# Chunked attention and gated feed-forward on one core: three tiles moved to transposing transfers, one load moved to another queue, a new order of loads, and eight equal blocks

## The chip, the core and the metric

The kernel runs on one core of one Trainium2 chip. The metric is the device time of one launch in microseconds (us). Each time is that of a whole execution; the profile shows one of them instruction by instruction.

## The reference

Two computations follow each other. The first is attention in chunks of 32 positions, for 4 batches, 8 heads, 768 positions and a head size of 64. A chunk sees 16 positions to its left, its own 32, 8 to its right, and 8 memory rows:

```python
for c in range(nc):
    l_start = max(0, c_start - left_ctx)          # 16
    r_end = min(S, c_end + right_ctx)             # 8
    k_full = np.concatenate([mem_k, k[:, :, l_start:r_end]], axis=2)
    v_full = np.concatenate([mem_v, v[:, :, l_start:r_end]], axis=2)
    scores = scale * np.matmul(q_c, k_full.transpose(0, 1, 3, 2))
    a = softmax(scores)
    out[:, :, c_start:c_end] = np.matmul(a, v_full)
```

The second takes the 3072 positions with their 512 features as `x` and gives the result:

```python
gate = np.maximum(x @ w_gate, 0.0)     # 512 -> 1536
val = x @ w_val
return (gate * val @ w_out).astype(np.float32)
```

## The kernel before

The 3072 positions are 24 tiles of 128 (`NT`), six to a batch (`TPB`). A tile goes through attention in these steps, whose names are the keys of the plan: `t` transposes q or k (TensorE, or a transposing transfer on SyncE's queue), `tc` or `kc` copies the result into place, `s` are the scores, `max`, `sub`, `exp`, `sum`, `rec`, `nrm` the softmax on VectorE and ScalarE, `p` transposes the probabilities, `pc` copies them out of PSUM, `v` multiplies with the values, and `x` copies the transposed attention result into `xT`, the input of the feed-forward part.

Tiles 0 to 5 load their q and k as three pairs (`load_pair`, names Q0 to K2); later tiles load them one by one (`load_qk`, names q6 to k23). `BY_DMA = (14, 15)` says from which tile on q and k are transposed by a transfer (`qk_dma`, L275) and no more by TensorE (`qk_t`, L266); `BY_DMA_P = 14` says it for p (`p_dma` L352, `p_t` L348). With a transfer, q lands in place, while k lands in a buffer `k_t` and is still copied by ScalarE. `scores` is L300, `values` L365.

The feed-forward part works on blocks of tiles: `BLOCKS` gives their sizes, seven blocks of three or four tiles. Within a block, `first` (L411) makes for each of twelve column groups `m` four products for the gate and four for the value; `relu` (ScalarE, L417) and `gate` (VectorE, L423) follow; then `second` (L432) makes twelve products for each tile, and the result is copied and stored. Blocks 0 and 1 are interleaved group by group while the weights still come.

Loads from memory that change the type go through GpSimd's queue in the order of the string `LOADS`: K and Q pairs, q and k, `v` with two digits (half of the chunks, head pair) for the values of batch 0, `b` with two digits (batch, head pair) for those of later batches, `w` for five groups of both weights, `o` for the output weights, `m` the memory values, `z` memsets of the second value buffer, `i` the identity matrix. The values lie in `v_bd`, of which there are two (`NSET`), used by batches in turn: batch 2 waits for the last values of batch 0, batch 3 for those of batch 1 (tile 11). The first half of batch 0's values comes by `v_parts` (L194), where the first chunk, which has no left context, is a load of its own.

The order of instructions on every engine is written by `schedule` (L704): a list plan with a duration for each step, priorities, and landing times for transfers. It only fixes orders; on the chip each instruction waits for what it needs. On one engine the instructions run in that order, so one that waits holds up those behind it. `LEAD` holds numbers that shape the priorities: entries 2 to 7 say how many column groups ahead of a block its attention may start (`pace`), the others order the copies of the memory pattern and the first tiles.

Of the kernel before, what the change touches and what calls it, by code (L numbers as in the profile page):

```python
# [16 lines left out]
ACT = mybir.ActivationFunctionType  # L17
# [4 lines left out]
def kernel(  # L22
# [12 lines left out]
    nc = tc.nc  # L35

    B, H, S, D = q.shape
    NMEM = mem_k.shape[2]
# [11 lines left out]
    KW = CH + NMEM  # L50
    CTX = 16 + CH + 8
    NSET = 2
    BLOCKS = [3, 3, 3, 4, 3, 4, 4]
    LEAD = [22, -5, 16, 12, 4, 3, 14, 23, 5, -6, 7, 17, 24, 4, 24, 12, 12, 0, 3, -6, -3]
    LAST = ((0, 384), (384, 512))
    BY_DMA = (14, 15)
    BY_DMA_P = 14
    LANDING = 3.0
    PAIRS = 3
    SPLIT = 1  # L60
# [2 lines left out]
    MEM_LEAD = (0,0,4,4)  # L63
    BY_DMA_X = 24
    BESIDE = 10.0
    LOADS = """K0 Q0 K1 i v01 Q1 Q2 K2 v00 v02 v03 w0 v12 w1 z1 v13 v11 w2 v10 w3
               m z3 w4 q7 q6 q8 z0 k8 k6 q9 k7 o1 k23 k9 o0 k13 z2 b13 b12 q13
               q21 k16 q12 b11 b10 k10 q17 k20 k11 q10 k18 q16 b21 q11 k15 q18 q14 k12 k14 b23
               b22 k21 k22 q15 b20 b30 q19 q20 q23 q22 b32 k17 b33 b31 k19"""

    KEY_RUNS = ((CH, KW, 0), (0, CH, NMEM), (KW, 64, KW))
    assert sum(BLOCKS) == NT and NMEM == 8 and D == 64 and H == 8
# [19 lines left out]
    def copy(eng, o, i):  # L92
        if eng is nc.scalar:
            nc.scalar.copy(o, i)  # L94
        else:
            eng.tensor_copy(o, i)
# [91 lines left out]
    def load_v_rows(b, par, hp, s0, s1, c0, c1):  # L188
# [2 lines left out]
            bass.AP(tensor=v.tensor, offset=v[b, 2 * hp + par, 0, 0].offset + (CH * c0 + s0 - 16) * D,  # L191
                    ap=[[D, s1 - s0], [CH * D, c1 - c0], [1, D]]))

    def v_parts(b, par, hp, c0, c1):  # L194
        parts = []
        if (b, par, hp, c0) == (0, 0, 0, 0):
            parts.append((b, par, hp, 16, CTX, 0, 1))
            c0 = 1
        if (b, par, hp, c1) == (B - 1, 1, HP - 1, NCH):
            c1 -= 1  # L200
            parts.append((b, par, hp, 0, 48, c1, c1 + 1))
        return parts + [(b, par, hp, 0, CTX, c0, c1)]
# [251 lines left out]
    def op(key, eng, fn, deps=(), prio=(0,), take=(), give=(), after=()):  # L454
        ops[key] = dict(eng=eng, fn=fn, deps=list(deps), prio=prio, take=list(take), give=list(give),
                        after=list(after))
# [4 lines left out]
    def psum(n):  # L461
# [3 lines left out]
    MARGIN = 1.2  # L465


    op("warm", {"DVE": 0.15}, lambda e: nc.vector.memset(warm, 0.0), prio=(-9,))
    op("warm2", {"ACT": 1.5}, lambda e: nc.scalar.activation(warm, warm, ACT.Exp), ["warm"], prio=(-9,), after=["vml"])  # L469
    op("vm00", {"DVE": 0.3}, lambda e: nc.vector.memset(vmem_0.rearrange("p h d -> p (h d)").bitcast(F32), 0.0),  # L470
       prio=(-8,), after=["im"])
    op("vml", {"ACT": 0.7}, lambda e: pattern_load(), prio=(-10,))
    op("kml", {"SP": 1.3}, lambda e: mem_load(), prio=(-8,))
    op("im", {"DVE": 0.12}, lambda e: nc.vector.memset(ident_h.bitcast(F32), 0.0), prio=(-8.5,), after=["warm"])
    op("ib", {"DVE": 0.25}, lambda e: nc.vector.tensor_copy(ident_b, ident_h), ["ident"], prio=(-7,))
# [45 lines left out]
    for a in range(NT):  # L521
# [52 lines left out]
        blk = block_of[a]  # L574
        j = a - starts[blk]
        ready = [("vl", b, 0 if b else t // 3, n) for n in range(2 * HP)]
        ready += [("mr", b, par, hp) for par in range(2) for hp in range(HP)] if b else []
        if a < BY_DMA_X:
            op(("v", a), {"PE": 0.41}, lambda e, a=a: values(a), [("pc", a)] + ready, (1, a, 10),
# [54 lines left out]
    def load_v_op(b, half, par, hp, c0, c1, deps, after):  # L634
        n = 2 * hp + par
        for i, part in enumerate(reversed(v_parts(b, par, hp, c0, c1))):
            rows = part[4] - part[3]
            load(("vl", b, half, n) if i == 0 else ("vx", b, n), rows * (part[6] - part[5]),
                 rows * (part[6] - part[5]) * 0.95e-3, lambda part=part: load_v_rows(*part), deps, (), after)

    def load_v_half(half, hp):
        c = NCH // 2
# [50 lines left out]
    def timed(d):  # L693
        return isinstance(d, tuple) and len(d) == 2 and isinstance(d[1], float)

    MOVE = {"t": 1.3, "p": 1.3, "x": 1.3, "mr": 0.7}

    LAG = 0.15

# [4 lines left out]
    def schedule():  # L704
# [30 lines left out]
        while len(started) < len(ops) + len(loads):  # L735
# [8 lines left out]
            while moved:  # L744
                moved = False
                for e in ("POOL", "PE", "ACT", "DVE", "SP"):
                    if free[e] > t + 1e-9:
                        continue
                    if e == "POOL":
                        if n_load == len(loads):  # L750
                            continue
                        o = loads[n_load]
                        if len(flying) >= 8 or not ready(o, t):
                            continue
                        n_load += 1
                        key = o["key"]
                        if o["n"]:
                            end = t + 0.62 + 0.27e-3 * o["n"]
                            queue_end = max(queue_end, end + 0.8) + o["work"]
                            load_end = queue_end + 1.0  # L760
                            flying.append(load_end)
                            done[key] = queue_end + (1.5 if n_load < 8 else 2.4 if n_load < 35 else 4.0)
                        else:
                            end = done[key] = t + o["work"]
                        if locked > t:
                            end += 0.25
                        fn = o["fn"]
                    else:
                        o = None
                        for _, key in todo[e]:  # L770
                            late_pe = e == "PE" and t > 36.0 and ops[key]["prio"][0] == 1
                            if ready(ops[key], t, MARGIN if late_pe else 0.0):
                                o = ops[key]
                                break
                        if o is None and e == "PE" and "ident" in done and 6.0 < t and ("f", 0, 0, 0) not in started:
                            order.append((t, idle_product))
                            free[e] = t + 0.1
                            heapq.heappush(times, free[e])
                            continue
                        if o is None:  # L780
                            continue
                        for x in o["eng"]:
                            todo[x].remove((o["prio"], key))
                        d = o["eng"][e] * (1.8 if e == "PE" and (t < 10.0 and key[0] == "t" or t < 24.0 and key[0] == "p") else 1.0)
                        if e == "DVE" and holds_port(key):
                            end = max(t + d, free["POOL"] + d - 0.1 if free["POOL"] > t else 0.0)
                            locked = end
                        else:
                            end = t + d
                        done[key] = end + (0.25 if e == "PE" else LAG)  # L790
                        if e == "SP" and key[0] in "tpx":
                            done[key] = end + (BESIDE if n_load < len(loads) or t < load_end else LANDING)
                        if e == "SP" and key[0] in MOVE:
                            queue_end = max(queue_end, t) + MOVE[key[0]]
                        fn = lambda o=o, e=e: o["fn"](e)
                        for g in o["give"]:
                            g, lag = g if isinstance(g, tuple) else (g, 0.0)
                            gives.append((done[key] + lag, g))
                            heapq.heappush(times, done[key] + lag)
# [47 lines left out]
```

## Time and profile before

| What | Value |
|---|---|
| Three runs | 239.75, 239.22, 237.85 us; median 239.22 |
| The profiled execution | 238.81 us, of which the span of the program is 237.0 |
| Granted TensorE clock | 1.00 |
| TensorE busy | 225.5 us, 2432 matmuls |
| VectorE busy | 150.9 us |
| ScalarE busy | 117.8 us |
| GpSimd busy | 91.5 us (issuing loads and setting memory) |
| Data moved by transfers | 27.17 MB |

The page of the profile gives the busy time of each engine, then the span in 40 slices with a digit for the busy tenths of each, then the queues, the chain of work that ended last, and groups of instructions by line, with the number of them, busy time, mean length, and the idle time of the engine before them with what ended it. A view by stage (windows) gives busy times between two moments. A view in order of time gives start and length of instructions; for matmuls the recorded length is more than the distance to the next, because they overlap.

### The profile page before, as it was taken

The page shows a single profiled execution, that of the slowest core. Times are in us where ns is not written, and L with a number is a line of the kernel's source. Part 1 is how long each engine was busy: PE and PEld are TensorE (multiplying, and loading weights), DVE is VectorE, ACT ScalarE, POOL GpSimd, SP SyncE. Part 2 cuts the span into 40 slices and gives each one's busy share as a digit, 9 for nine tenths or more (in the row PEclk, how much of TensorE's full clock was granted, in tenths as well). Part 3 has the DMA queues.
Part 4 walks back from the last instruction along what each step waited for, and adds up shares of the span by engine and source line. Part 5 has one row for each costly group of instructions (what it writes and reads, how often), then busy time and mean ns, then how long its engine had stood idle before and what let it go on. Part 6 is the DMA issues. An engine that isn't in the chain of part 4 may idle for free.

```text
span 237.0 us, 5892 instructions
## 1 busy us (share of the span) xinstructions
PE 225.5 (95%) x2432; PEld 125.6 (53%) x2432; DVE 150.9 (64%) x267; ACT 117.8 (50%) x251; POOL 91.5 (39%) x107
## 2 busy tenths in 40 slices
PE   0988989999999999999999999999999999999994
PEld 0777655665544666655444545664454444444442
DVE  5789953468999789954999146797775520234300
ACT  7988735444442786653643356655553331333212
POOL 6989998884875787059430000000000000000000
PEclk9999999999999999999999999999999999999999
DMA  7999999999999999979999344545420002200022
GB/s 75 163 160 179 161 180 179 165 192 172 151 174 211 199 179 133 118 127 149 141 150 117 75 149 111 69 46 121 127 48 0 0 4 88 88 0 0 3 88 89
DMA packets 121147, 27.17 MB, mean 115 GB/s; under 512 B 111264, under 2 KB 118176, under 8 KB 121120
## 3 DMA queue, kind: packets, MB, share of 16 engines
q0 software_dynamic: 101376, 16.61, 94.7%
q1 hardware_dynamic: 19664, 10.16, 18.5%
q8 instruction: 19, 0.31, 0.6%
q14 instruction: 8, 0.07, 0.1%
q10 hardware_dynamic: 80, 0.02, 0.0%
HBM read 33.24 MB, written 6.29 MB: 167 GB/s over the span
## 4 chain that ended last, share of the span: by engine, by line
PE 84%; POOL 8%; DMA 3%; ACT 2%; issue 1%; ACTq 0%; POOLq 0%
PE out_ps L432 26%; PE v_ps L411 25%; PE g_ps L411 25%; POOL v_bd L189 5%; PE xT_ps L365 4%; DMA v_bd<-in_v_dram 3%; PE s_ps L300 2%; PE qk_ps L266 2%; POOL w_gate_sb L121 1%; POOL w_val_sb L121 1%; POOL qk_p L220 1%; PE pT_ps L348 1%; ACT v_bd L94 1%; POOL v_bd L135 1%; ACT L469 1%
## 5 line engine op out<-in xcount | busy, mean ns | idle before, releaser
L423 DVE TENSOR_TENSOR gvT<-v_ps,g_relu 128x384 f16<-128x384 f32 (+1 forms) x84 | 51.2, 610 | 42.4 <-PE v_ps L411 42.0
L411 PE MATMUL v_ps<-xT,w_val_sb 128*128 128x384 f16 (+1 forms) x336 | 75.9, 349 | 0.3 <-DMA w_val_sb<-in_moe_w_val_dram 0.3
L411 PE MATMUL g_ps<-xT,w_gate_sb 128*128 128x384 f16 (+1 forms) x336 | 75.9, 349 | 0.0
L417 ACT ACTIVATE g_relu<-g_ps 128x384 f16<-128x384 f32 (+1 forms) x84 | 44.8, 534 | 57.9 <-PE g_ps L411 47.4
L432 PE MATMUL out_ps<-w_out_sb,gvT 128*128 128x512 f16 (+2 forms) x300 | 65.5, 370 | 0.0
L411 PEld LDWEIGHTS <-w_gate_sb 128*128 128x128 f16 x336 | 32.1, 98 | 28.1 <-DMA w_gate_sb<-in_moe_w_gate_dram 0.4
L411 PEld LDWEIGHTS <-w_val_sb 128*128 128x128 f16 x336 | 31.3, 98 | 26.8 <-DMA w_val_sb<-in_moe_w_val_dram 0.5
L189 POOL DMA_DIRECT2D v_bd<-in_v_dram x42 | 37.7, 910 | 16.6 <-PE xT_ps L365 9.3
L432 PEld LDWEIGHTS <-gvT 128*128 128x128 f16 x300 | 28.0, 98 | 30.0
L94 ACT COPY o_sb<-out_ps 128x512 f32<-128x512 f32 (+2 forms) x25 | 14.2, 569 | 32.8 <-PE out_ps L432 32.4
L164 DVE TENSOR_TENSOR v_bd<-vmem 8x768 int32<-8x768 int32 (+1 forms) x29 | 26.6, 944 | 1.1 <-ACT vmem L94 0.9
L327 ACT ACTIVATE p_exp<-dif 128x64 f16<-128x64 f32 (+2 forms) x72 | 19.6, 336 | 8.9 <-DVE dif L320 8.7
L313 DVE TENSOR_REDUCE mx<-s_ps 128x8 f32<-128x512 f32 x24 | 16.3, 677 | 5.5 <-PE s_ps L300 5.2
L331 DVE TENSOR_REDUCE sm<-p_exp 128x8 f32<-128x512 f16 x24 | 16.3, 678 | 5.2 <-ACT p_exp L327 5.1
L211 POOL DMA_DIRECT2D qk_b<-in_k_dram x18 | 16.0, 891 | 5.5 <-DMA w_out_sb<-in_moe_w_out_dram 2.8
L211 POOL DMA_DIRECT2D qk_b<-in_q_dram x18 | 16.0, 902 | 5.0 <-DMA v_bd<-in_v_dram 1.6
L342 DVE TENSOR_TENSOR p_n<-p_exp,rinv 128x512 f16<-128x512 f16 x24 | 16.4, 684 | 0.3
L320 DVE TENSOR_TENSOR dif<-s_ps,mx 128x512 f32<-128x512 f32 x24 | 16.4, 682 | 0.1
L365 PEld LDWEIGHTS <-v_bd 128*128 128x128 f16 x384 | 12.7, 96 | 5.2 <-issue 1.3
L365 PE MATMUL xT_ps<-pT,v_bd 128*128 128x32 f16 x384 | 13.0, 176 | 0.9 <-DMA v_bd<-in_v_dram 0.7
L94 ACT CAST xT<-xT_ps 128x512 f16<-128x512 f32 x17 | 9.9, 587 | 7.3 <-PE xT_ps L365 7.0
L403 PE MATMUL idle_ps<-ident_h 128*128 128x128 f16 x87 | 8.4, 238 | 4.8 <-POOL ident_h masks.py:199 4.8
(46 smaller groups left out, 125.5 us busy)
## 6 DMA issues: line engine op xcount, KB each, us to landing
out_dram<-o_sb SPq DMA_DIRECT2D x23, 256.0 KB, 2.1
v_bd<-in_v_dram POOLq DMA_DIRECT2D x23, 168.0 KB, 9.6
qk_b<-in_q_dram POOLq DMA_DIRECT2D x18, 128.0 KB, 9.3
qk_b<-in_k_dram POOLq DMA_DIRECT2D x18, 128.0 KB, 9.2
w_out_sb<-in_moe_w_out_dram POOLq DMA_DIRECT2D x2, 768.0 KB, 10.8
v_bd<-in_v_dram POOLq DMA_DIRECT2D x15, 84.0 KB, 4.9
qk_p<-in_k_dram POOLq DMA_DIRECT2D x3, 256.0 KB, 5.9
qk_p<-in_q_dram POOLq DMA_DIRECT2D x3, 256.0 KB, 5.3
```

The lines of the kernel that those rows point to most:

```text
L94: nc.scalar.copy(o, i)
L164: nc.vector.tensor_tensor(out=o, in0=i, in1=i, op=ALU.bitwise_or)
L189: nc.gpsimd.dma_start(v_bd[b % NSET][64 * par + NMEM + s0:64 * par + NMEM + s1, hp, c0:c1, D * par:D * par + D], bass.AP(tensor=v.tensor, ...
L211: nc.gpsimd.dma_start(qk_b[a, i], bass.AP(tensor=x.tensor, offset=x[b, 0, 128 * t, 0].offset, ap=[[D, 128], [S * D, H], [1, D]]))
L320: nc.vector.tensor_tensor(out=SM[a, "dif"].rearrange("p h r s -> p r h s"), in0=S_ps.pop(a), in1=mx_b, op=ALU.subtract)
L327: nc.scalar.activation(p[:, :, :, s0:s0 + k1 - k0], dif[:, :, :, k0:k1], ACT.Exp, scale=SCALE)
L342: nc.vector.tensor_tensor(out=P_n[a], in0=SM.pop((a, "p")), in1=rinv_b, op=ALU.mult)
L365: nc.tensor.matmul(ps[:, hp, r], lhsT=v_bd[b % NSET][:, hp, 4 * t + g, :], rhs=x[:, hp, r], start=True, stop=True)
L411: nc.tensor.matmul(ps, lhsT=w[:, f, 128 * m:128 * m + 128], rhs=xTs[blk][:, f, :], start=(f == 0), stop=(f == NFC - 1))
L417: nc.scalar.activation(st["r", m], st.pop((0, m)), ACT.Relu)
L423: nc.vector.tensor_tensor(out=st["gv"][:, m, :], in0=st.pop((1, m)), in1=st.pop(("r", m)), op=ALU.mult)
L432: nc.tensor.matmul(st["o", t, cols], lhsT=st["gv"][:, m, 128 * t:128 * t + 128], rhs=w_out_sb[:, m, slice(*cols)], start=(m == 0), stop=(m ...
```

## The change

- `BLOCKS` becomes eight blocks of three tiles.
- `BY_DMA` becomes (13, 13) and `BY_DMA_P` 12: q of tile 13, k of tiles 13 and 14, and p of tiles 12 and 13 are transposed by transfers on SyncE's queue.
- The first chunk's 40 rows of v for head 0 come as float32 by SyncE's queue (`load_first`) into rows 24 to 63 of `vmem_f`, the buffer that already takes the memory rows; a memset clears rows 0 to 31 before (`vf0`), and a copy on ScalarE or VectorE (`vfc`) writes rows 0 to 63 into the first chunk of `v_bd`. GpSimd's load of these rows is gone. The load of the memory rows and the memset `warm` now come after `vf0`; the values of tile 0 wait for `vfc`.
- The plan assumes later landing: 2.7 us in place of 2.4 after a load's turn in the queue (for loads 8 to 34), transposing transfers that take 1.45 in place of 1.3 of queue time, rows of v 1.0 in place of 0.95 ns per row, and a load that counts as in flight until 0.2 us after its assumed landing.
- `LOADS` and `LEAD` hold other orders and numbers.

```diff
-    BLOCKS = [3, 3, 3, 4, 3, 4, 4]
-    LEAD = [22, -5, 16, 12, 4, 3, 14, 23, 5, -6, 7, 17, 24, 4, 24, 12, 12, 0, 3, -6, -3]
+    BLOCKS = [3, 3, 3, 3, 3, 3, 3, 3]
+    LEAD = [24, 8, 20, 20, 11, 11, 4, 7, 10, 5, 4, 24, 17, 0, 24, 3, 22, 1, -6, -6, 7]
...
-    BY_DMA = (14, 15)
-    BY_DMA_P = 14
+    BY_DMA = (13, 13)
+    BY_DMA_P = 12
...
-    LOADS = """K0 Q0 K1 i v01 Q1 Q2 K2 v00 v02 v03 w0 v12 w1 z1 v13 v11 w2 v10 w3
-               m z3 w4 q7 q6 q8 z0 k8 k6 q9 k7 o1 k23 k9 o0 k13 z2 b13 b12 q13
-               q21 k16 q12 b11 b10 k10 q17 k20 k11 q10 k18 q16 b21 q11 k15 q18 q14 k12 k14 b23
-               b22 k21 k22 q15 b20 b30 q19 q20 q23 q22 b32 k17 b33 b31 k19"""
+    LOADS = """K0 Q0 i K1 K2 Q1 v01 v00 Q2 v11 v03 v02 w0 v13 v12 w1 v10 w2 q6 k7
+               w3 z2 z3 z1 q7 k6 b12 m k8 q9 w4 k16 o0 q8 k9 o1 b11 z0 q10 q17
+               k23 k15 k10 b10 b13 k19 k14 k11 q11 k13 k18 q15 q14 k12 q13 k17 q20 q12 b21 b22
+               q21 k22 k21 k20 q19 b33 b20 b23 q16 b32 q18 b31 q23 b30 q22"""
...
+    def load_first():
+        nc.sync.dma_start(
+            vmem_f[NMEM + 16:64, 0, 0:D],
+            bass.AP(tensor=v.tensor, offset=v[0, 0, 0, 0].offset, ap=[[D, 64 - NMEM - 16], [1, D]]))
...
         if (b, par, hp, c0) == (0, 0, 0, 0):
-            parts.append((b, par, hp, 16, CTX, 0, 1))
             c0 = 1
...
-    op("warm", {"DVE": 0.15}, lambda e: nc.vector.memset(warm, 0.0), prio=(-9,))
+    op("vf0", {"DVE": 0.1}, lambda e: nc.vector.memset(vmem_f[0:32, 0, 0:D], 0.0), prio=(-10,))
+    op("warm", {"DVE": 0.15}, lambda e: nc.vector.memset(warm, 0.0), prio=(-9,), after=["vf0"])
...
+    op("vfl", {"SP": 0.4}, lambda e: load_first(), ["vf0"], prio=(-7.5,), after=["kml"])
+    op("vfc", {"ACT": 0.15, "DVE": 0.15}, lambda e: copy(engine[e], v_bd[0][0:64, 0, 0, 0:D], vmem_f[0:64, 0, 0:D]),
+       [("vfl", 3.2), ("vml", 1.2), ("spread", 0, 0)], prio=(1, 0, 9))
...
-    op("vml", {"ACT": 0.7}, lambda e: pattern_load(), prio=(-10,))
+    op("vml", {"ACT": 0.7}, lambda e: pattern_load(), ["vf0"], prio=(-10,))
...
+        ready += ["vfc"] if a == 0 else []
...
-                 rows * (part[6] - part[5]) * 0.95e-3, lambda part=part: load_v_rows(*part), deps, (), after)
+                 rows * (part[6] - part[5]) * 1.0e-3, lambda part=part: load_v_rows(*part), deps, (), after)
...
-    MOVE = {"t": 1.3, "p": 1.3, "x": 1.3, "mr": 0.7}
+    MOVE = {"t": 1.45, "p": 1.45, "x": 1.3, "mr": 0.7}
...
-                            flying.append(load_end)
-                            done[key] = queue_end + (1.5 if n_load < 8 else 2.4 if n_load < 35 else 4.0)
+                            done[key] = queue_end + (1.5 if n_load < 8 else 2.7 if n_load < 35 else 4.0)
+                            flying.append(done[key] + 0.2)
```

## The prediction

> **What bounds the kernel now.** I read the page first, then the busy times by stage, then TensorE's instructions in order of time, and last GpSimd's issues and the transfers' landing times.
>
> ```profile
> span 237.0 us, 5892 instructions
> PE 225.5 (95%) x2432; PEld 125.6 (53%) x2432; DVE 150.9 (64%) x267; ACT 117.8 (50%) x251; POOL 91.5 (39%) x107
> PE   0988989999999999999999999999999999999994
> DMA  7999999999999999979999344545420002200022
> PE 84%; POOL 8%; DMA 3%; ACT 2%; issue 1%; ACTq 0%; POOLq 0%
> ```
>
> TensorE (PE) is busy 95% of the span, in every slice after the start, and 84% of the chain that ended last is PE. The transfers stand at nine tenths with one dip up to the 22nd slice of 5.9 us, so until about 130 us they are loaded too, but hidden. The stages:
>
> ```profile
> core 0: us, PE busy (x) PEld busy (x) DVE busy (x) ACT busy (x) POOL busy (x), PEclk, DMA share, GB/s
> 79.60:109.20 29.60, 29.60 (x410) 18.30 (x408) 21.73 (x45) 20.06 (x46) 17.24 (x20) 1.00 1.88 142
> 109.20:142.50 33.30, 33.30 (x290) 15.78 (x288) 23.62 (x36) 14.33 (x30) 8.05 (x9) 1.00 1.43 133
> 202.60:233.70 31.10, 31.10 (x156) 14.65 (x154) 8.30 (x12) 9.99 (x17) 0.00 (x0) 1.00 0.09 34
> 233.70:237.00 3.30, 0.01 (x1) 0.00 (x0) 0.00 (x0) 0.27 (x1) 0.00 (x0) 1.00 0.23 79
> ```
>
> PE has no idle record in any of these stages; 3.3 us of copy and store close the span. Since ends of matmuls are modelled, I test this with the distance from start to start:
>
> ```profile
> 80.78 0.39 PE L266 MATMUL qk_ps<-ident_b,qk_b 128*128 128x128 bf16 x4
> 81.00 0.81 PE L411 MATMUL g_ps<-xT,w_gate_sb 128*128 128x384 f16 x4
> 81.75 0.31 PE L300 MATMUL s_ps<-kT,qT 64*32 64x64 bf16 x32
> 81.99 0.40 PE L266 MATMUL qk_ps<-ident_b,qk_b 128*128 128x128 bf16 x4
> 88.44 0.39 PE L348 MATMUL pT_ps<-ident_h,p_n 128*128 128x128 f16 x4
> 88.66 0.81 PE L411 MATMUL v_ps<-xT,w_val_sb 128*128 128x384 f16 x4
> 89.31 0.81 PE L411 MATMUL g_ps<-xT,w_gate_sb 128*128 128x384 f16 x4
> 100.06 2.75 PE L432 MATMUL out_ps<-w_out_sb,gvT 128*128 128x512 f16 x12
> 102.64 0.56 PE L365 MATMUL xT_ps<-pT,v_bd 128*128 128x32 f16 x16
> 103.05 0.38 PE L348 MATMUL pT_ps<-ident_h,p_n 128*128 128x128 f16 x4
> 113.27 1.03 PE L411 MATMUL g_ps<-xT,w_gate_sb 128*128 128x512 f16 x4
> 114.14 1.03 PE L411 MATMUL v_ps<-xT,w_val_sb 128*128 128x512 f16 x4
> ```
>
> Four transposes of q, k or p hold PE 0.22 us (80.78 to 81.00, 88.44 to 88.66); the 32 products of scores 0.24; those of values 0.41; four first products of a three-tile block 0.65, of a four-tile block 0.87; twelve second products 2.58. Stage 79.6 to 109.2 is one three-tile block with, by its 410 records, 5 scores, 4 values and 13 sets of transposes beside it: 24 x 0.65 + 3 x 2.58 + 5 x 0.24 + 4 x 0.41 + 13 x 0.22 = 15.6 + 7.7 + 1.2 + 1.6 + 2.9 = 29.0 of its 29.6 us. So about 0.6 us of a stage is lost, and the four-tile stage after it, by the same prices (24 x 0.87 + 4 x 2.58 + 3 x 0.24 + 3 x 0.41 = 33.2 of 33.3), loses nothing. **PE's work is the bound, and the order of the instructions wastes almost none of it.** Only three things can move the end: less work on PE, an earlier start, or new waits.
>
> **The change, part by part.** (1) *Transposes.* The limits go from 14, 15 and 14 to 13, 13 and 12: q of tile 13, k of tiles 13 and 14 (two, not one) and p of tiles 12 and 13 leave PE. That is five sets of four, 5 x 0.22 = **-1.1 us** on the path. The least is what is left if such a set stands where PE waits anyway, 0; the most is 5 x 0.39 (the recorded length of a set) = -1.95. I take the start distance, since the next instruction does start after it. With them go three copies out of PSUM (q, and p twice) on engines that are not the bound; the two copies of k stay, from another source.
>
> [...]
>
> SP gets five more transposing transfers (29 to 34). What they cost is landing time and load on the transfer engines:
>
> ```profile
> DMA to landing us min/median/max: 2.4/2.8/10.0
> 148.00:163.00 15.00, 15.00 (x237) 8.90 (x236) 13.34 (x27) 8.70 (x23) 0.00 (x0) 1.00 0.46 63
> ```
>
> k's transfers took from 2.4 to 10.0 us to land; the five new ones fall beside loads, before 130 us, so I count with the long end. From 148 to 163 us only transposing transfers ran, eight by SP's timeline, at a share of 0.46, so one is 0.46 x 15 / 8 = 0.86 us of transfer time; five are 4.3 us, which at the share of loaded stages (1.6 and more) moves the last load some 2.6 us back. That costs nothing while scores and values stand late enough in PE's order. They do by need: with blocks of three, tiles 12 to 14 are first used by the block that starts at about 132 us (79.6 plus two stages of 25 to 27), where before tile 12 was used at 109.2. The cover is PE's own backlog of first products; where it is too short, PE waits in order, and all products behind it wait too. Bounds 0 and +5 us (half the 10.0 us), value **+0.5**, near nothing, because the due time is some 20 us later.
>
> (2) *Eight blocks of three.* First products: now 4 x 24 x 0.65 + 3 x 24 x 0.87 = 125.0, then 8 x 24 x 0.65 = 124.8; second products stay. On the path -0.2 to +0.2 by the rounding: **0**. VectorE's and ScalarE's share:
>
> ```profile
> L423 DVE TENSOR_TENSOR gvT<-v_ps,g_relu 128x384 f16<-128x384 f32 x48 | 26.4, 551 | 10.9 <-PE v_ps L411 10.7
> L423 DVE TENSOR_TENSOR gvT<-v_ps,g_relu 128x512 f16<-128x512 f32 x36 | 24.8, 689 | 31.5 <-PE v_ps L411 31.3
> ```
>
> VectorE pays 96 x 0.551 instead of 26.4 + 24.8, +1.7 us; it hides under PE, whose pair of products takes 1.30 us against 0.55 for the gate. What gets thinner is slack: PE can run one pair ahead, so a gate may come 1.30 us late in a three-tile block, 1.73 in a four-tile one. An attention step or two of VectorE ahead of it use that up. The three-tile stage above lost 0.6 us and the four-tile one nothing; two more such stages with attention beside them make **+0.5**, bounds 0 and +1.5.
>
> [...]
>
> (3) *First chunk of v by SP, and the order of the loads.* The start:
>
> ```profile
> 0.85 0.11 DVE L474 MEMSET ident_h<- 128x64 f32 x1
> 24.23 0.81 PE L411 MATMUL g_ps<-xT,w_gate_sb 128*128 128x384 f16 x4
> 31.40 0.82 PE L411 MATMUL v_ps<-xT,w_val_sb 128*128 128x384 f16 x4 [0.29 <-DMA w_val_sb<-in_moe_w_val_dram]
> 33.57 0.98 PE L365 MATMUL xT_ps<-pT,v_bd 128*128 128x32 f16 x32 [0.70 <-DMA v_bd<-in_v_dram]
> 6.97 1.80 POOL L220 DMA_DIRECT2D qk_p<-in_q_dram  x2
> 18.99 0.78 POOL L121 DMA_DIRECT2D w_gate_sb<-in_moe_w_gate_dram  x1
> 20.51 1.40 POOL L135 MEMSET v_bd<- 128x1536 f32 x1
> 26.48 1.65 POOL L189 DMA_DIRECT2D v_bd<-in_v_dram  x2
> 32.30 0.87 POOL L121 DMA_DIRECT2D w_gate_sb<-in_moe_w_gate_dram  x1
> w_gate_sb<-in_moe_w_gate_dram POOLq DMA_DIRECT2D x3, 256.0 KB, 5.1
> w_gate_sb<-in_moe_w_gate_dram POOLq DMA_DIRECT2D x2, 384.0 KB, 7.6
> ```
>
> The first product starts at 24.23; then PE waits 0.29 us for weights and 0.70 for the last rows of v (issued at 26.48): 1.0 us that could go. GpSimd issues about one load per 0.8 us without pause, so places in its list are times. One issue goes to SP, 0.8 us less for GpSimd; the new memset (as small as the 0.11 us one shown) and the copy of 64 rows (estimated from it at 0.1 to 0.3) go to VectorE or ACT, and the pattern's load on ACT now waits for the memset, some 0.3 us. k and q of the second pair stand closer to the front (Q1 from 6.97 to about 5.6). The last v half (v10) goes from places 28 and 29 to 25 and 26, and the 1.40 us memset in front of it moves back: 26.48 - 3 x 0.8 - 1.4 = 22.7, so the 0.70 us wait ends. Late next is the second weight group: places 20 and 21 become 23 and 24, 18.99 + 2.4 less 0.7 (a stall of GpSimd early on that goes) = 20.7, with 0.8 for its pair and 5.1 to land 26.6 to 27.1; it is wanted after four sets, 24.23 + 2.6 = 26.8: a wait of 0 to 0.3. After it the fifth group: now issued at 32.30, then behind three memsets and eight loads, about 40; its landing at 7.6 or more is 48 to 50, wanted after 36 sets of 0.65 and some 3 us of attention, about 50.5. So nearly all the gain stays if attention is not itself later: **-0.9**. Bounds: -2.4 (both waits and 1.4 us for the earlier Q1) and +1.6 (both waits stay and the second group comes 0.6 late).
>
> (4) *Landing times of the plan.* They issue nothing; they only move instructions within PE's, ACT's and VectorE's order. A later assumed landing means fewer waits in order and later attention; its price is in (1) to (3).
>
> **Sum.** -1.1 + 0.5 + 0 + 0.5 - 0.9 = -1.0 us. The profiled execution took 238.81 us (span 237.0 and 1.8 around it): 237.8. The median of the three runs, 239.22, is 0.4 above it; I leave the forecast at 237.8.
>
> **The rivals.** *A, earlier start:* Q1 and the third pair are there sooner, the first product moves to about 22.8 and both waits go: -1.1 - 2.4 + 0.7 for the stages = -2.8, **236.0**. For it: five of the six loads of q and k pairs now stand ahead of all of v. Against: the weights come by the same list of issues, so a product that starts sooner only waits there.
>
> *B, values wait for v of batch 2 (slower):*
>
> ```profile
> 92.08 2.00 POOL L189 DMA_DIRECT2D v_bd<-in_v_dram  x2
> 103.42 1.94 POOL L189 DMA_DIRECT2D v_bd<-in_v_dram  x2 [9.34 <-PE xT_ps L365]
> v_bd<-in_v_dram POOLq DMA_DIRECT2D x23, 168.0 KB, 9.6
> ```
>
> GpSimd now sits 9.34 us until the values of tile 11 free the buffer for batch 3; all of batch 2's v was issued by 92.08 + 2. In the new list b33 stands ahead of b20 and b23. So the last v of batch 2 is issued after that release and seven issues of 1.0 us, and lands 9.6 us after: 103.4 + 7 + 9.6 = 120, and the five transposes beside it push it by up to 2.6. Tile 12's values stood at 110 us; if PE's order has them before about 121, PE stops there with all products behind. It decides from there on, and costs the difference: 4 to 6 us at 115 to 117, so 237.8 + 4.5 = **242.3**. Against it: the need is at 132, eleven us after.
>
> *C, start not better:* the second or fifth weight group comes late and takes back what v gives, and the stages lose their 1 us: -1.1 + 1.0 + 0.6 = +0.5, **239.3**, no difference.
>
> [...]
>
> **How the numbers follow.** Forecast 0.38, A 0.23, B 0.24, C 0.12, D 0.03. A measurement of this kernel tells about 1%, 2.4 us, from no change: under 236.8 or over 241.6 beside the median. Faster takes 0.19 of A and 0.06 of the forecast: 0.25. Slower takes 0.19 of B and 0.04 of C, where the late weights add up: 0.23. The rest, 0.52, is within 1%. Forecast alone: 236.6 to 239.2. The range for 8 in 10 goes from 235.2 (A with the larger bound of the transposes) to 242.0 (into B).
>
> **What would show it.** In the changed profile: sets of q and k transposes 68 to 56 matmuls, p 56 to 48; transposing transfers 34; all first products 128x384, 768 of them; v issues on GpSimd 41. Step (1) is right if PE shows no wait between 100 and 140 us; wrong if PE waits for a transposed tile or v there. Step (2) is right if PE's sets in the m loops stay 0.65 apart, wrong if they wait on VectorE. Step (3) is right if no wait for v_bd remains near 30 us and the first product starts at 23.5 to 24.5. A first product after 25 us, or a wait of over 2 us after 40 us, makes the forecast wrong.

## The result and the profile after

| | Before | After |
|---|---|---|
| Median, 15 runs each | 239.22 us | 236.89 us |
| Lowest and highest | 237.85 to 242.69 | 236.36 to 240.55 |
| Profiled execution | 238.81 us | 236.48 us |
| Its span | 237.0 us | 234.7 us |

The medians differ by 2.33 us, and the two profiled executions by the same; this is just inside the 1% that the prediction called no change, and the median is 0.9 us below its forecast. The ratio is 0.9924, with a 95% interval of 0.9898 to 0.995; it compares means of the fast executions (14 on each side), and by it the gain is 1.8 us. These rows of the page of the kernel after answer to those shown of before:

```profile
PE 223.3 (95%) x2514; PEld 132.3 (56%) x2514; DVE 151.3 (64%) x278; ACT 120.4 (51%) x263; POOL 90.5 (39%) x106
DMA  7999999999999999999999942551212210120012
PE 91%; DVE 6%; ACT 1%; issue 1%; ACTq 0%
```

PE is still the bound, now with 91% of the chain that ended last instead of 84%: 8% of GpSimd and 3% of transfers have left it, and 6% of VectorE (DVE) have come in, all ahead of the first product. The transfers' dip in the 18th slice has gone; they stay at nine tenths to the 23rd. (PE's count rises because blocks of three need 96 more first products, smaller ones.) The counts that the prediction named are there: 56 transposes of q and k and 48 of p on PE, 768 first products, 34 transposing transfers and 41 issues of v. All waits of PE that the waits view lists:

```profile
PE qk_ps L236 <- DVE kmem_b L96: 6.2, 1, 6.2
PE s_ps L304 <- ACT qT L94: 0.7, 1, 0.7
PE s_ps L304 <- DVE dif L324: 0.7, 1, 0.7
PE s_ps L304 <- DVE rinv L339: 0.4, 1, 0.4
PE pT_ps L352 <- DVE p_n L346: 0.2, 1, 0.2
PE xT_ps L369 <- ACT pT L94: 0.2, 1, 0.2
```

In order of time all of them lie before 25 us. After the first product there is none. One stage by windows, and PE's records around the new start:

```profile
79.20:106.84 27.64, 27.64 (x368) 16.01 (x365) 21.45 (x42) 15.06 (x36) 17.62 (x19) 1.00 2.16 150
...
24.36 0.40 PE L352 MATMUL pT_ps<-ident_h,p_n 128*128 128x128 f16 x4 [0.19 <-DVE p_n L346]
25.10 0.81 PE L415 MATMUL g_ps<-xT,w_gate_sb 128*128 128x384 f16 x4
36.30 0.81 PE L415 MATMUL g_ps<-xT,w_gate_sb 128*128 128x384 f16 x4
```

**Where 2.3 us came from.** I count sets of four first products in both. Before, the 1st starts at 24.23 and the 15th at 36.92, with three sets of p and the values of three tiles between. After, they start at 25.10 and 36.30, with two sets of p, the values of three tiles and two sets of q, k between. So the start is 0.87 us *later*, and at the 15th set PE is 0.62 us ahead, with two sets of q, k done that before still had to come (0.44; the p at 24.36 is one of the three that before did later). That is 1.06 us by 36 us, all other work being equal at that point. Of the other 1.24 us, five sets of transposes at 0.22 are 1.1; 0.14 is left for all else.

### The profile page after: what moved, and what is told of

Its sections match the earlier page's. It is cut to its first block, busy times and chain, and to the rows that moved or that the text cites. A ratio compares the mean times of both kernels' runs of the same rounds, so it can differ in the third digit from the quotient of the medians.

```text
span 234.7 us, 6122 instructions
## 1 busy us (share of the span) xinstructions
PE 223.3 (95%) x2514; PEld 132.3 (56%) x2514; DVE 151.3 (64%) x278; ACT 120.4 (51%) x263; POOL 90.5 (39%) x106
## 4 chain that ended last, share of the span: by engine, by line
PE 91%; DVE 6%; ACT 1%; issue 1%; ACTq 0%
PE v_ps L415 27%; PE g_ps L415 27%; PE out_ps L436 27%; PE xT_ps L369 4%; PE s_ps L304 2%; PE qk_ps L270 1%; DVE mx L317 1%; PE qk_ps L236 1%; DVE dif L324 1%; DVE p_n L346 1%; DVE sm L335 1%; PE pT_ps L352 1%; PE idle_ps L407 1%; ACT L474 1%; DVE v_bd L164 0%
## 5 line engine op out<-in xcount | busy, mean ns | idle before, releaser
L427 DVE TENSOR_TENSOR gvT<-v_ps,g_relu 128x384 f16<-128x384 f32 x96 | 53.2, 554 | 55.3 <-PE v_ps L415 49.6
L415 PE MATMUL v_ps<-xT,w_val_sb 128*128 128x384 f16 x384 | 78.1, 326 | 0.0
L415 PE MATMUL g_ps<-xT,w_gate_sb 128*128 128x384 f16 x384 | 78.1, 326 | 0.0
L421 ACT ACTIVATE g_relu<-g_ps 128x384 f16<-128x384 f32 x96 | 47.0, 490 | 50.8 <-DVE gvT L427 25.7
L415 PEld LDWEIGHTS <-w_gate_sb 128*128 128x128 f16 x384 | 36.5, 98 | 23.2
L415 PEld LDWEIGHTS <-w_val_sb 128*128 128x128 f16 x384 | 36.1, 98 | 22.5
L189 POOL DMA_DIRECT2D v_bd<-in_v_dram x41 | 37.1, 913 | 13.6 <-DMA v_bd<-in_v_dram 6.6
L164 DVE TENSOR_TENSOR v_bd<-vmem 8x768 int32<-8x768 int32 (+1 forms) x28 | 26.0, 945 | 0.4
L94 ACT CAST xT<-xT_ps 128x512 f16<-128x512 f32 x21 | 12.1, 585 | 9.9 <-PE xT_ps L369 9.6
L369 PEld LDWEIGHTS <-v_bd 128*128 128x128 f16 x384 | 12.3, 96 | 3.1 <-issue 0.3
L236 PE MATMUL qk_ps<-ident_b,qk_p 128*64 128x128 bf16 x96 | 5.3, 274 | 6.2 <-DVE kmem_b L96 6.2
## 6 DMA issues: line engine op xcount, KB each, us to landing
v_bd<-in_v_dram POOLq DMA_DIRECT2D x23, 168.0 KB, 12.9
w_out_sb<-in_moe_w_out_dram POOLq DMA_DIRECT2D x2, 768.0 KB, 12.3
```

Of the source, the lines that this page charges most:

```text
L164: nc.vector.tensor_tensor(out=o, in0=i, in1=i, op=ALU.bitwise_or)
L189: nc.gpsimd.dma_start(v_bd[b % NSET][64 * par + NMEM + s0:64 * par + NMEM + s1, hp, c0:c1, D * par:D * par + D], bass.AP(tensor=v.tensor, ...
L369: nc.tensor.matmul(ps[:, hp, r], lhsT=v_bd[b % NSET][:, hp, 4 * t + g, :], rhs=x[:, hp, r], start=True, stop=True)
L415: nc.tensor.matmul(ps, lhsT=w[:, f, 128 * m:128 * m + 128], rhs=xTs[blk][:, f, :], start=(f == 0), stop=(f == NFC - 1))
L421: nc.scalar.activation(st["r", m], st.pop((0, m)), ACT.Relu)
L427: nc.vector.tensor_tensor(out=st["gv"][:, m, :], in0=st.pop((1, m)), in1=st.pop(("r", m)), op=ALU.mult)
```

## The experiments

Each median stands against the kernel before, run on the same chip (239.13 to 239.37), and, where it helps, against 236.89. T stands for the five sets that the change transposes by transfers. The ratios go by means. Measured from the mean of the kernel after in place of its median, the differences to it come out up to 1.0 us smaller: kernel 3's 1.25 becomes 0.8, kernel 1's 1.86 becomes 1.3.

| Kernel | Median us (runs) | Ratio to before, interval | Span us |
|---|---|---|---|
| 1 after, ten sets doubled | 238.75 (12) | 0.9979, 0.996 to 0.9998 | 237.0 |
| 2 before, with T | 246.04 (6) | 1.0266, 1.0225 to 1.0306 | 243.0 |
| 3 after, without T | 238.14 (10) | 0.9958, 0.9934 to 0.9982 | 236.3 |
| 4 after, mixed blocks | 250.31 (6) | 1.0445, 1.0398 to 1.0492 | 247.7 |
| 5 before, with the new start | 238.24 (11) | 0.9961, 0.9946 to 0.9976 | 236.5 |
| 6 after, first chunk by GpSimd | 238.17 (12) | 0.9956, 0.9933 to 0.9979 | 235.5 |
| 7 after, old landing times | 239.05 (12) | 1.0007, 0.9985 to 1.0029 | 237.2 |
| 8 after, more T | 239.34 (12) | 1.0018, 0.9986 to 1.0049 | 237.4 |
| 9 as 4, b20 and b23 ahead | 247.81 (6) | 1.0364, 1.0321 to 1.0408 | 246.6 |
| 10 after, q, k of tile 12 by T | 240.23 (12) | 1.0032, 1.0004 to 1.006 | 238.5 |
| 11 as 8, 22 load buffers | 239.61 (12) | 1.0035, 1.0014 to 1.0057 | 239.5 |
| 12 mixed blocks, without T | 244.26 (6) | 1.0218, 1.0183 to 1.0254 | 241.0 |

One thing holds for all: the plan is written anew for each kernel, so a change of one number also moves instructions elsewhere. Where a row shows such a move, I say so.

### What is one set of transposes worth?

**1.** Doubling ten sets of four (p of tiles 6 to 11; q, k of 6 and 7):

```diff
-        for hp in range(HP):
+        for hp in [h for _ in range(2 if 6 <= a < 8 else 1) for h in range(HP)]:
...
-        for hp in range(HP):
+        for hp in [h for _ in range(2 if 6 <= a < 12 else 1) for h in range(HP)]:
```

> The changed kernel with ten sets of four TensorE transposes done twice (p of tiles 6 to 11, q and k of tiles 6 and 7), each into the place it writes anyway; nothing else moves. If TensorE is the bound and a set holds it for the 0.22 us from start to start, the time rises by 10 x 0.22 = 2.2 us, to 239.1. If such sets stand where TensorE waits anyway, it rises by 0 to 0.5. [...]

The median rose by 1.86 us, the span by 2.3: 0.19 to 0.23 per set. A doubled set in the order of time:

```profile
82.36 0.61 PE L352 MATMUL pT_ps<-ident_h,p_n 128*128 128x128 f16 x8
82.80 0.81 PE L415 MATMUL g_ps<-xT,w_gate_sb 128*128 128x384 f16 x4
```

Eight take 0.44 us from start to start. The price of term (1) stands; this run gives about 50 ns for each transpose.

**3.** Only the limits back to 14, 15 and 14, in the kernel after:

```diff
-    BY_DMA = (13, 13)
-    BY_DMA_P = 12
+    BY_DMA = (14, 15)
+    BY_DMA_P = 14
```

> The changed kernel with the three limits set back to 14, 15 and 14. If the five sets are 1.1 us of the gain: 238.0, 1.1 above the changed kernel. If the gain lies in the blocks or the start alone: 236.9 as the changed kernel.

It was 1.25 us slower than after (span +1.6; 0.8 by means): five sets at 0.25. PE again has no wait after 25 us. So in blocks of three the transfers cost nothing beside them.

### What hides the transposing transfers?

**2.** The same five sets by transfer in the kernel *before*, with its blocks, loads and landing times:

```diff
-    BY_DMA = (14, 15)
-    BY_DMA_P = 14
+    BY_DMA = (13, 13)
+    BY_DMA_P = 12
```

> The kernel before with the three limits alone set to 13, 13 and 12. If the five sets are what the change gives on TensorE, 1.1 us less than before, 238.1. The rival: with before's blocks tile 12 is needed by the block at 109 us, so its transposing transfers come between: TensorE waits, and the time is 0 to 4 us above before (239 to 243).

Neither: it lost 6.8 us. PE in order of time:

```profile
111.57 0.57 PE L365 MATMUL xT_ps<-pT,v_bd 128*128 128x32 f16 x16 [2.77 <-DMA pT<-p_n]
112.81 1.02 PE L411 MATMUL g_ps<-xT,w_gate_sb 128*128 128x512 f16 x4 [0.67 <-ACT xT L94]
113.67 1.68 PE L411 MATMUL v_ps<-xT,w_val_sb 128*128 128x512 f16 x4
115.14 1.91 PE L411 MATMUL g_ps<-xT,w_gate_sb 128*128 128x512 f16 x4
116.98 0.41 PE L300 MATMUL s_ps<-kT,qT 64*32 64x64 bf16 x32
```

p of tile 12 lands 2.77 us late at the border of the block that holds tiles 9 to 12, xT follows 0.67 us late, and the next two sets take 1.47 and 1.84 us instead of 0.87 (113.67 to 115.14 to 116.98). So to 3.4 us of waits come 1.6 us in slow sets; the granted clock is 0.50 from 113.9 to 117.3 us. Three further waits are new or longer beside before, one of them the second of the two in the last row (0.77 us at 175.67):

```profile
PE g_ps L411 <- DMA w_gate_sb<-in_moe_w_gate_dram: 1.1, 1, 1.1
PE qk_ps L266 <- DMA qk_b<-in_k_dram: 0.9, 1, 0.9
PE g_ps L411 <- ACT xT L94: 1.4, 2, 0.8
```

3.4 + 1.6 + 1.1 + 0.9 + 0.8, less 1.1 for the five sets, 0.7 for the wait for v that is gone here and 0.3 for an earlier first product (23.96), is 5.7 of the 6.0 us by which the span grew.

**4.** The kernel after with the old blocks, all else kept:

```diff
-    BLOCKS = [3, 3, 3, 3, 3, 3, 3, 3]
+    BLOCKS = [3, 3, 3, 4, 3, 4, 4]
```

> The changed kernel with the blocks of before (3, 3, 3, 4, 3, 4, 4); the lead numbers stay. If blocks of three are worth nothing on TensorE (0.65 and 0.87 us a set, the same per tile): 236.9, within 0.5 of the changed kernel. The rival, that equal blocks give the slack which hides the five transfers: 238 to 241, with a wait of TensorE for a transposed tile or for v between 95 and 130 us.

13.4 us slower than after. PE in order of time, then the window around it:

```profile
115.47 0.52 PE L369 MATMUL xT_ps<-pT,v_bd 128*128 128x32 f16 x12 [7.75 <-DMA v_bd<-in_v_dram]
118.69 0.69 PE L369 MATMUL xT_ps<-pT,v_bd 128*128 128x32 f16 x20 [2.70 <-DMA v_bd<-in_v_dram]
119.63 1.86 PE L415 MATMUL g_ps<-xT,w_gate_sb 128*128 128x512 f16 x4 [0.25 <-ACT xT L94]
122.89 1.03 PE L415 MATMUL g_ps<-xT,w_gate_sb 128*128 128x512 f16 x4
...
112.60:122.70 10.10, 4.28 (x40) 2.23 (x41) 4.71 (x7) 2.42 (x4) 4.78 (x6) 0.50 2.05 163
```

The values of tile 12 wait 7.75 and 2.70 us for v of batch 2. This is rival B, at its place, with the blocks that need tile 12 a stage earlier. The granted clock is 0.50 in that window, which holds the end of the first wait, the second wait and the products behind it; the two sets from 119.63 take 3.26 us instead of 1.74.

**9.** Rival B's reason was that b33 stands ahead of b20 and b23. In kernel 4 they change places:

```diff
-               q21 k22 k21 k20 q19 b33 b20 b23 q16 b32 q18 b31 q23 b30 q22"""
+               q21 k22 k21 k20 q19 b20 b23 b33 q16 b32 q18 b31 q23 b30 q22"""
```

> The changed kernel with before's blocks (as in the run with 250.31 us) and, besides, the loads b20 and b23 moved ahead of b33, so that v of batch 2 does not queue behind the release by tile 11. If these loads are the wait of 10.4 us, it goes: 237 to 241, with 0 to 3 us of wait left for the transposing transfer of tile 12's p. If the mixed blocks themselves cost the time: 248 to 250.

```profile
114.11 0.48 PE L369 MATMUL xT_ps<-pT,v_bd 128*128 128x32 f16 x12 [6.36 <-DMA v_bd<-in_v_dram]
117.39 0.27 PE L369 MATMUL xT_ps<-pT,v_bd 128*128 128x32 f16 x4 [2.80 <-DMA v_bd<-in_v_dram]
```

The waits fall from 10.45 to 9.16 us, the span by 1.1, the median by 2.5. So the order of b33 is a small part. Nor is it the release by tile 11, on which B's sum was built. GpSimd's load of b33 in the kernel after:

```profile
96.23 2.02 POOL L189 DMA_DIRECT2D v_bd<-in_v_dram  x2 [0.27 <-PE xT_ps L369]
```

For batch 3's v GpSimd waits 0.27 us where it waited 9.34, and in kernels 4 and 9 it doesn't wait for it at all. What does delay v, kernel 12 shows.

**12.** Mixed blocks, after's loads, and no T:

```diff
-    BLOCKS = [3, 3, 3, 3, 3, 3, 3, 3]
+    BLOCKS = [3, 3, 3, 4, 3, 4, 4]
...
-    BY_DMA = (13, 13)
-    BY_DMA_P = 12
+    BY_DMA = (14, 15)
+    BY_DMA_P = 14
```

> The kernel after with blocks of 3, 3, 3, 4, 3, 4, 4 tiles, and with p of tiles 12 and 13 and q, k of tile 13 transposed on PE again. With the mixed blocks and the transposing transfers the time was 250.3, with 10.5 us of waits for v of batch 2. Theory 1: the transfers hold the load buffers and so make the v late; without the five sets of them the wait is 2 us or less, and the time is 238 to 240. Theory 2: the list itself, with these blocks' due times, puts the v of batch 2 late: 5 to 10 us of waits at the values of tile 12 stay, and the time is 244 to 249.

```profile
108.89 0.32 PE L304 MATMUL s_ps<-kT,qT 64*32 64x64 bf16 x32 [1.08 <-DVE dif L324]
111.63 0.68 PE L369 MATMUL xT_ps<-pT,v_bd 128*128 128x32 f16 x20 [1.95 <-DMA v_bd<-in_v_dram]
112.99 1.86 PE L415 MATMUL g_ps<-xT,w_gate_sb 128*128 128x512 f16 x4 [0.68 <-ACT xT L94]
115.89 1.03 PE L415 MATMUL g_ps<-xT,w_gate_sb 128*128 128x512 f16 x4
```

Each theory got half: the wait for v is 1.95 us, as the first one said, but the median is 244.26, at the second one's lower end (the profiled execution, 242.77, is the fastest of the six). That execution is placed: waits of 1.08, 1.95 and 0.68 us, and two sets in 2.90 us (112.99 to 115.89) instead of 1.74, are 4.9; less 1.0 for the start, 3.9 of the 4.0 us that its span lies above before's. So the list by itself does put mixed blocks' tile 12 late, by less than with T. (The wait for v may cost nothing here: in the profile the chain to the product at 112.99 runs through VectorE's softmax steps and `xT`, not through that load.)

How T makes v late can be read by laying kernel 4 beside it. In each fence the first rows are of kernel 4 and the last of kernel 12. GpSimd's longest wait for a transposing transfer, which holds a load buffer until it lands:

```profile
89.86 0.87 POOL L215 DMA_DIRECT2D qk_b<-in_k_dram  x1 [2.99 <-DMA k_t<-qk_b]
...
89.25 1.77 POOL L215 DMA_DIRECT2D qk_b<-in_k_dram  x2 [4.19 <-DMA qT<-qk_b]
```

The landing of the four loads that bring b20 and b23, and SyncE's transposing transfers near them:

```profile
DMA to landing us min/median/max: 10.6/12.3/13.5
99.84 1.39 SPq L356 DMA_TRANSPOSE pT<-p_n  x1
105.91 1.27 SPq L279 DMA_TRANSPOSE qT<-qk_b  x1
...
DMA to landing us min/median/max: 7.1/7.3/8.0
112.99 1.31 SPq L356 DMA_TRANSPOSE pT<-p_n  x1
```

Theory 1's mechanism is not it: GpSimd waits for held buffers in both, 6.8 us in all in kernel 4 and 6.5 in kernel 12. The loads themselves are slower. The last one is issued at 105.02 and takes 13.5 us in kernel 4, at 103.45 and 8.0 us in kernel 12: 5.5 of the 7 us between the two landings are landing time. In kernel 4 SyncE issues four transposing transfers between 99.84 and 105.91, in kernel 12 none between 89.84 and 112.99. So T's transfers run beside v, and v lands later; why by so much is not shown. In blocks of three it is the same (all 23 loads of v of 168 KB take 8.5 us in the median in kernel 3, 12.9 in the kernel after), but there the values come after the landing.

With kernels 3, 4 and after, kernel 12 gives a square, all with the new loads:

| | T by PE | T by transfer |
|---|---|---|
| Mixed blocks | 244.26 | 250.31 |
| Blocks of three | 238.14 | 236.89 |

The same transfers cost 6.05 us in mixed blocks (6.8 in kernel 2, with the old loads) and bring 1.25 in blocks of three. The blocks decide it: the block that first uses tile 12 begins at 109.1 us in the kernel before and at 131.8 in the kernel after.

### The start and the landing times

**5.** The kernel before with only the new start: the list of loads up to w4, the first chunk by SP, the later landing times, and entries 8 to 20 of `LEAD`. The core of it:

```diff
-    LOADS = """K0 Q0 K1 i v01 Q1 Q2 K2 v00 v02 v03 w0 v12 w1 z1 v13 v11 w2 v10 w3
-               m z3 w4 q7 q6 q8 z0 k8 k6 q9 k7 o1 k23 k9 o0 k13 z2 b13 b12 q13
+    LOADS = """K0 Q0 i K1 K2 Q1 v01 v00 Q2 v11 v03 v02 w0 v13 v12 w1 v10 w2 q6 k7
+               w3 z2 z3 z1 q7 k6 b12 m k8 q9 w4 q8 z0 o1 k23 k9 o0 k13 b13 q13
...
+    op("vfl", {"SP": 0.4}, lambda e: load_first(), ["vf0"], prio=(-7.5,), after=["kml"])
...
-    MOVE = {"t": 1.3, "p": 1.3, "x": 1.3, "mr": 0.7}
+    MOVE = {"t": 1.45, "p": 1.45, "x": 1.3, "mr": 0.7}
```

> The kernel before with only the start of the changed one: its list of loads up to the fifth weight group (the rest in the old order), the first chunk of v by SP, the landing numbers and the lead numbers 8 to 20; blocks and transposes stay as before. If the start gives what the trace of the changed kernel shows (first product 0.9 later, 1.6 us of waits between 24 and 34 us gone, one set of transposes more done ahead): -0.9 to -1.3, 238.1. If the new landing numbers or the order upset the later stages: 239 to 243, with waits after 80 us. If the gain of the changed kernel were all in blocks and transposes: 239.2.

1.0 us faster than before. Its first product starts at 25.06, and PE waits for neither v nor weights from 25 to 40 us. The start (−1.0, kernel 5) and T in blocks of three (−1.25, kernel 3) add up to −2.25 of the −2.33 (by means, −0.9 and −0.8 of −1.8). Kernel 5 holds the new landing times too, so its −1.0 is not the price of the loads alone. Kernels 5 and 3 differ in the blocks, in the rest of `LOADS`, and in entries 0 to 7 of `LEAD`, and by only 0.1 us in time: without more transfers the blocks, with that list and those entries, are worth nothing.

**6.** Only the first chunk's rows back on GpSimd:

```diff
+            parts.append((b, par, hp, 16, CTX, 0, 1))
...
-    op("vfl", {"SP": 0.4}, lambda e: load_first(), ["vf0"], prio=(-7.5,), after=["kml"])
-    op("vfc", {"ACT": 0.15, "DVE": 0.15}, lambda e: copy(engine[e], v_bd[0][0:64, 0, 0, 0:D], vmem_f[0:64, 0, 0:D]),
```

> The changed kernel with the first chunk's rows of v again as a load of GpSimd (no memset and no copy for it). If GpSimd's list sets the start, 0.8 us more in front of the weights: 0.5 to 0.8 above the changed kernel, 237.5. If VectorE's chain of softmax steps sets the start, the memset and the copy go from it and GpSimd's extra issue is hidden: 236.4 to 236.9.

+1.3 us in the median, +0.8 in the span.

```profile
24.95 0.81 PE L416 MATMUL g_ps<-xT,w_gate_sb 128*128 128x384 f16 x4 [0.47 <-DVE xT L96]
25.60 0.39 PE L353 MATMUL pT_ps<-ident_h,p_n 128*128 128x128 f16 x4
25.92 0.31 PE L305 MATMUL s_ps<-kT,qT 64*32 64x64 bf16 x32
```

The first product is not later than after's (25.10), but a set of p and the scores of a tile now stand behind it, 0.5 us that after did before it. So the load on SP pays, though not by an earlier first product. By 40 us PE has done one set of four first products less than after, with all other work equal: 0.65 us, and it keeps about this distance to the end. That is most of the span's 0.8; the median's 1.3 stays open.

**7.** Only the numbers for landing back:

```diff
-    MOVE = {"t": 1.45, "p": 1.45, "x": 1.3, "mr": 0.7}
+    MOVE = {"t": 1.3, "p": 1.3, "x": 1.3, "mr": 0.7}
...
-                            done[key] = queue_end + (1.5 if n_load < 8 else 2.7 if n_load < 35 else 4.0)
-                            flying.append(done[key] + 0.2)
+                            flying.append(load_end)
+                            done[key] = queue_end + (1.5 if n_load < 8 else 2.4 if n_load < 35 else 4.0)
```

> The changed kernel with the landing numbers of before (2.4, 1.3, 0.95, in flight until 1.0 after the queue's end). If they only shift orders where slack is: 236.9, within 0.5. If the earlier assumed landing puts scores or values ahead of their transfers, TensorE waits between 25 and 60 us: 238 to 240.

2.2 us slower than after: nothing is left of the gain. The first row is of the kernel after, the others of kernel 7:

```profile
119.54 0.95 PE L369 MATMUL xT_ps<-pT,v_bd 128*128 128x32 f16 x32
...
116.50 0.45 PE L369 MATMUL xT_ps<-pT,v_bd 128*128 128x32 f16 x12
118.47 0.25 PE L369 MATMUL xT_ps<-pT,v_bd 128*128 128x32 f16 x4 [1.51 <-DMA v_bd<-in_v_dram]
```

The earlier assumed landing puts the values of tile 12 some 3 us sooner in PE's order (116.50), and the last of them wait 1.51 us for v of batch 2. After's own stand at 119.54 and wait for nothing: the last load of batch 2's v is issued at 103.23, takes 14.7 us and has landed 1.6 us before. So after misses rival B by less than two us, and these numbers are what makes it miss. The rest of kernel 7's loss comes early: by 44 us PE has done five first products less than after, 0.8 us, with a wait of 0.44 us for `xT` at 35.86. The second theory had named that place, but not the larger wait at 118.47.

### Would more transfers be better still?

**8, 10, 11.** The kernel after with q, k of tile 12 and p of tiles 10 and 11 too (8); the same but p from tile 12 as in after (10); and as 8 with 22 instead of 16 buffers for loaded q and k (11):

```diff
-    BY_DMA = (13, 13)
-    BY_DMA_P = 12
+    BY_DMA = (12, 12)
+    BY_DMA_P = 10
```
```diff
-    BY_DMA_P = 10
+    BY_DMA_P = 12
```
```diff
-    ldpool = ctx.enter_context(tc.tile_pool(name="ldpool", bufs=16))
+    ldpool = ctx.enter_context(tc.tile_pool(name="ldpool", bufs=22))
```

> The changed kernel with four more sets by transfer: limits 12, 12 and p from 10 (q and k of tile 12, p of tiles 10 and 11). If TensorE's work is the bound and the new landings still have slack, -4 x 0.22 = -0.9: 236.0. If the slack that the blocks give ends here, since tiles 10 and 11 are needed by the block that starts at 106.8 us and p takes up to 9.6 us to land: a wait of 2 to 6 us before 110 us, 239 to 243.

> The changed kernel with two more sets by transfer: q and k from tile 12, p as it is. If landings have slack, -2 x 0.22 = -0.4: 236.5. If the transfers of tile 12, between 77 and 92 us, hold up the buffers of q and k and with them GpSimd's list, v of batch 2 lands later and TensorE waits near 119 us: 237.5 to 240.

> The kernel after, with q and k of tiles 12 and 13, and p of tiles 10 to 13, by transposing transfers (as in the run with more of them), and with 22 instead of 16 buffers for loaded q and k. Theory 1: the transposing transfers hold load buffers until they land, GpSimd's loop waits for them (2.0 and 2.5 us at 89.8 and 93.2 us in the kernel after), and its later transfers land late; with six more buffers those waits go, the transfers land in time, and the removed sets of PE transposes count at 0.2 us each: 236.0 to 237. Theory 2: the waits are for the transposing transfers themselves, which land late beside the loads, whatever the buffers: the waits of 0.9 to 1.4 us on p and q stay, and the time is 238.5 to 240.

They were 2.5, 3.3 and 2.7 us slower than after. PE's waits, two rows of kernel 8 and then two of kernel 11:

```profile
107.51 0.82 PE L415 MATMUL g_ps<-xT,w_gate_sb 128*128 128x384 f16 x4 [1.02 <-DVE xT L96]
134.31 0.32 PE L304 MATMUL s_ps<-kT,qT 64*32 64x64 bf16 x32 [1.37 <-DMA qT<-qk_b]
...
108.24 1.46 PE L415 MATMUL g_ps<-xT,w_gate_sb 128*128 128x384 f16 x4 [1.02 <-DVE xT L96]
136.35 0.32 PE L304 MATMUL s_ps<-kT,qT 64*32 64x64 bf16 x32 [1.37 <-DMA qT<-qk_b]
```

The waits are the same 1.02 and 1.37 us (and 0.85 before them, in both) with 16 and 22 buffers, though with 22 GpSimd no longer waits for any transposing transfer. So the buffers are not what stops this step. In kernel 8 the three waits are 3.2 us; less 0.9 for four more sets, that is most of the 2.7 by which its span exceeds after's. The 1.37 is a q landing late; the other two stand at a block's border, where PE has no first products left to run meanwhile. (Kernel 11's profiled execution, 241.25, is the slowest of its twelve.) Kernel 10 waits 1.75 us for the scores at 134.4, not near 119 as one theory had it, and its start came 1.4 us later in the profile (first product at 26.47), a move of the plan. None beats the kernel after.

## Why the prediction was right, and where not

**The bound.** "PE's work is the bound, and the order of the instructions wastes almost none of it" held: less work on PE and fewer waits make up the whole difference.

**(1) Transposes, −1.1.** Right by kernel 1 (0.19 to 0.23 a set) and kernel 3 (1.25 for five). The allowance of +0.5 for landing was 0. Its reasoning, that the need comes later with blocks of three, is what the square shows; but the bound if that cover is gone, "Bounds 0 and +5 us", was too small: 6.05 and 6.8 us (kernel 4 against 12, 2 against before), each net of the gain. It priced the late landing of the transposed tiles, which is the 2.77 us in kernel 2, and not what comes with it: loads of v beside the transfers that take 12.3 us to land in place of 7.3 (kernels 4 and 12), and sets at a granted clock of 0.50 after a wait (kernels 2 and 4). Nor was the cover 20 us: the values of tile 12 moved from 105.86 to 119.54, some 14 us, since attention runs ahead of its block.

**(2) Blocks of three.** PE 0 was right: kernels 3 and 5, which differ in the rest of the list too, are 0.1 apart. The allowance of +0.5 for thinner slack on VectorE was mis-sized: no wait on VectorE after 25 us. The stage from 79.20 us, by its counts of instructions and the prediction's prices, is 24 x 0.65 + 3 x 2.58 + 5 x 0.24 + 3 x 0.41 + 7 x 0.22 = 27.3 of 27.64 us: 0.3 lost where the stage before lost 0.6. The granted clock stands at 1.00 in that stage.

**(3) Start, −0.9.** The sum was right (−1.06 by the count, −1.0 by kernel 5), the makeup not. The prediction let the first product start at 23.5 to 24.5; it starts at 25.10, and it named "A first product after 25 us" as making the forecast wrong. It did not, because with the start later by 0.87 us came the end of all waits behind it and one more set of p ahead of it; the test was set on the wrong quantity. The waits of 0.29 and 0.70 us that it listed are gone.

Its times for the loads came out: the last half of v is issued at 22.52 (forecast 22.7), the second weight group at 21.00 (20.7), the fifth at 39.89 (40), although the early stall of GpSimd that was to go is still there (0.87 us at 7.00). What it missed is that the loads no longer set the start. Rows of the chain that ended last, first of before, then of the kernel after:

```profile
27.30 6.14 DMA v_bd<-in_v_dram
33.57 0.98 PE xT_ps L365 x32
...
23.61 0.70 DVE p_n L346
24.36 0.40 PE pT_ps L352 x4
```

Before, the chain goes by GpSimd's issues and the landing of v to the values at 33.57. After, it is VectorE's softmax steps, from 14.4 to 24.3 us one behind the other with at most 0.02 us between them, then p of a further tile, which the new order puts ahead of the first product, its scores, and the product. ScalarE's copy of `xT` for that product ends at 24.84, just before. The chain is read from the profile; no run makes VectorE's steps shorter to test it. The plan's landing times belong to this start too (kernel 7).

**(4) Landing times of the plan.** "They issue nothing" is true, and "its price is in (1) to (3)" was wrong: kernel 7 puts 2.2 us on them. They keep the values of tile 12 behind v of batch 2, which is 1.5 us, and give 0.8 us of the start.

**The sum.** −1.0 forecast, −2.33 measured: the two terms of work were right to 0.3 us together, and the two allowances of +0.5, which no row of before priced directly, are most of the miss.

**The rivals.** B named the right place; its price of 4 to 6 us is about half of the 10.45 us of waits in kernel 4, and its cause, the order of b33 and the release by tile 11, was wrong (kernel 9, GpSimd's 0.27 us). It put tile 12's values of before at 110 us; they stood at 105.86, and 109.94 is tile 13's. Its distance was judged as eleven us and is under two, since the plan runs the attention of tile 12 well ahead of its block. A's 236.0 is as near the median as the forecast's 237.8, but its mechanism, a first product at 22.8, did not happen: that nearness is luck. C falls: the weights are in time, and the five sets count (1.25 us in kernel 3).

## What to carry to other kernels

Where one engine runs without a gap, count sets of the same instruction from start to start between two fixed points of both traces; the moment of the first says little by itself. Work taken off that engine brings its start-to-start time (here 0.22 us a set) only while what replaces it is due late: the same five sets were worth −1.25 or +6 us by the size of the blocks. Assumed landing times in a plan are part of the change, to be priced like an instruction: the margin they guard here is under two us.

## What the hardware showed that I had not expected

After waits on TensorE its products ran slower in some profiles. In kernel 4, with waits of 7.75 and 2.70 us, the granted clock was 0.50 from 112.6 to 122.7 us, and two sets took 3.26 us instead of 1.74; in kernel 2, after 2.77 and 0.67 us, it was 0.50 from 113.9 to 117.3 us, and two sets took 3.31 instead of 1.74. Over the whole spans the granted clocks were 0.979 and 0.993. This does not follow every such wait. Kernels 8 and 11 have the same two waits of 0.85 and 1.02 us shortly before these windows, and the clock (third number from the end) is 1.00 in the one and 0.51 in the other:

```profile
107.60:111.00 3.40, 3.40 (x52) 1.93 (x52) 3.29 (x7) 2.14 (x6) 3.40 (x5) 1.00 1.36 84
107.60:111.00 3.40, 2.76 (x24) 1.13 (x32) 2.69 (x5) 1.21 (x6) 3.40 (x4) 0.51 1.21 174
```

What decides between them, no run here shows. Transposing transfers beside loads were slow. In the kernel after, the fourteen of q and k that SyncE issued from 75 to 130 us took 7.3 to 9.4 us from issue to landing, at a DMA share of 1.98 to 2.16; the seven from 143.9 us on, after the last load, took 2.4 to 4.2 at a share of 0.39. Medians of all:

```profile
k_t<-qk_b SPq DMA_TRANSPOSE x11, 7.8
qT<-qk_b SPq DMA_TRANSPOSE x11, 7.7
```
